# Attention in front of a mixture of experts: flat key tiles, and softmax sums from a column of ones

## The chip, the cores and the metric

The kernel runs on one core of one Trainium2 chip. The metric is the device time of one execution in microseconds (us), the median of several runs. Names of engines: PE is TensorE, PEld its weight loads, DVE VectorE, ACT ScalarE, POOL GpSimd, SP SyncE, which here only issues DMAs.

## What is computed

Batch 4, 8 heads, 576 positions, head dimension 64; then a mixture of 8 experts over the 2304 tokens of width 512, with hidden width 1024 and one expert per token.

```
scores = q @ k^T / 8 + bias(i, j, head)      # bias: a small MLP of the positions alone
attn   = exp(scores - max);  attn = attn / (sum(attn) + 1e-09)
x      = attn @ v                            # reshaped to tokens x 512
e      = argmax of normalised x @ normalised expert_emb^T / tau
out    = gate * (relu(x @ w1[e]) @ w2[e])
```

The change lies in the attention alone: in how the keys are laid out and scaled, in how the row sums of the exponentials are formed, and in the numbers by which the order of the work is set.

## The kernel before

**Units.** The four batches are taken in two pairs (`pr`). Queries come in five chunks per pair: chunks 0 to 3 hold 128 queries of each batch, chunk 4 the 64 left over. A unit is one pair, one chunk and one head; the order is pair 0 with chunks 4, 0, 1, 2, 3, then pair 1 with chunks 0, 1, 2, 3, 4, each with 8 heads: 80 units. In chunk 4 two heads make one step (`two`), so there are 64 steps of full chunks and 8 double steps. A step (`unit`, L659) is: scores of both batches on PE (L692, 12 matmuls of 16 bit pieces, into PSUM tiles `s0` and `s1`), bias add with row extremum on DVE (L707), the exponential on ACT (L710), 9 transposes on PE (L721) with copies out of PSUM on ACT or DVE (L727), the product with the values on PE (L743, 40 matmul halves into PSUM tile `o`), and division by the sums on DVE.

**Sums.** In full chunks the exponential's instruction also adds up its row into `sums`; every second unit DVE adds 1e-9 and takes the reciprocal (L753, L754), which needs the exponentials alone, and then multiplies two units' products at once (L759). In chunk 4 the value tile's 65th column, which holds ones in all chunks (L464), is used: the product is 65 wide and its last column is the sum (L748 to L750). `o` is one PSUM bank with one buffer; a new one is begun every four units (L731), so it holds four units of 128 columns, or in chunk 4 two double steps of 130.

**Keys.** `load_k` brings keys of 4 heads and a batch pair in 10 DMAs into `kr`, 9 blocks of 64 columns: batch 0's four full blocks of 128 keys, batch 1's four, which begin at key 64, and a shared block with batch 0's last 64 keys and batch 1's first 64. There is one such buffer, filled four times (pair by half of the heads). `prep_k` takes the greatest magnitude (two reductions, L493, over 4 and 5 blocks), makes a power of two per head of it (L495 to L490), and per head writes an upper 16 bit piece (ACT, L514 and L516) and a lower one (DVE, three instructions at L520) into `khl`, in which the shared block stands twice. Ten transposes (L528) and one copy of 1280 columns (L531) make `kt`. For batch 1 the scores of its first 64 keys go to columns 448 to 511 of `s1`, the rest to 512 to 1023 (L688 to L692).

**Order.** All of this is handed to a list scheduler (`Sched`, L123) that runs when the kernel is built. Each operation has an engine or a choice of engines, an assumed duration, what it reads and writes, and a priority counted in units; the planner places operations by time and priority and writes each engine's queue in that order. The priorities are numbers at the file's head: `KLA`, `KLB`, `KHB`, `KH`, `KP0`, `KP1` for the keys' preparation, `KA`, `KB`, `QA`, `VA` for when loads may start, `oS` to `oX` for the parts of a unit, `oL` for the bias tiles' loads, `BL` to `BP0` for the making of the bias, `PACE` for how far loads may run ahead of the DMA queue, `PEN` for what a copy on DVE must gain over ACT, `FP`, `FQ`, `FINP`, `FINE`, `GEP` for the end of attention. `BBK` says how many steps of the bias of chunk 0 may use four PSUM banks in place of one.

Three parts of the whole follow each other: up to some 150 us the bias of all chunks is made beside the first units (L618 on DVE, L633 on PE); from there units alone up to some 367 us, with the second pair's keys prepared up to 234 us; then the tokens are dispatched and the experts run.

```
k = (2 * D + 2) * (u % 4 // 2) if two else 128 * (u % 4)
nc.scalar.activation(pp()[:, S_ * b:S_ * b + S_], sx(), AF.Exp, bias=mx()[:, b:b + 1], scale=-1.0, accum_out=None if two else sums()[:, h, b:b + 1])
```

Of the kernel before, what the change touches and what calls it, by code (L numbers as in the profile page):

```python
# [27 lines left out]
S_ = S  # L28
# [22 lines left out]
BBK = 6  # L51
KBS = 12
KA = 21
KB = 35
QA = 36
VA = 11
KLA = 9.369
KLB = 5.845
KHB = 0.818
KP0 = -5.658  # L60
KP1 = -3.883
KH = 5.81
QL1 = 9.937
QL0 = 51.383
BL1 = 12.618
BS1 = 1.935
BP0 = -10.567
PSB = 0
ALPHA = 20.886
# [3 lines left out]
PRLD = 90.243  # L73
# [17 lines left out]
STP, STPM = 12.256, 60.738  # L91
VP0 = 127.364
oL0 = -2.201
# [170 lines left out]
class Kern:  # L264
# [97 lines left out]
    def attention(self):  # L362
        with ExitStack() as tail, ExitStack() as cx:
# [13 lines left out]
            for n in ("sm_kz", "sm_wt", "sm_sums", "sm_mx", "sm_ri"):  # L377
                self.p[n], self.r[n] = self.p[n.split("_")[0]], Rot(sizes[n.split("_")[0]])
# [3 lines left out]
            self.d, self.banks_used = {}, 0  # L382

# [54 lines left out]
    def load_kv(self, src, pr, hh, t, tok, prio, after, apart=0):  # L438
        nc = self.nc
        hs = slice(4 * hh, 4 * hh + 4)  # L440
        for b in range(2):
            a = src[2 * pr + b, hs]

            def main(c, a=a, b=b):
                nc.sync.dma_start(t()[:, :, 4 * b + c, 0:D], a[:, 64 * b + 128 * c:64 * b + 128 * c + 128, :].rearrange("h p d -> p h d"))

            def tail(a=a, b=b):
                nc.sync.dma_start(t()[64 * b:64 * b + 64, :, 8 + b * apart, 0:D], a[:, 512 - 512 * b:576 - 512 * b, :].rearrange("h p d -> p h d"))

            for c in range(4):  # L450
                self.S.op([("SP", 550, lambda c=c, main=main: main(c))], [], [tok] + ([] if b else [tok + (0,)]), [t], prio, 600, after, PACE if after else None)
            self.S.op([("SP", 550, tail)], [], [tok], [t], prio, 365, after, PACE if after else None)

    def load_k(self, pr, hh, prio, after):
        t = self.d["kr", pr, hh] = self.buf("kr", [128, 4, 9, 64], pool="kraw")
        self.load_kv(self.i["k"], pr, hh, t, ("kr", pr, hh), prio, after)

    def load_v(self, pr, hh, prio, after):

        nc = self.nc  # L460
        t = self.d["v", pr, hh] = self.buf("v", [128, 4, 10, D + 1])

        def zero():
            nc.gpsimd.memset(t()[:, :, :, D], 1.0)  # L464
            nc.gpsimd.memset(t()[0:64, :, 9, :], 0.0)
            nc.gpsimd.memset(t()[64:128, :, 8, :], 0.0)

        self.S.op([("POOL", 600, zero)], [], [("v", pr, hh)], [t], prio, 0, after)
        self.load_kv(self.i["v"], pr, hh, t, ("v", pr, hh), prio, after, 1)

    def prep_k(self, pr, hh, prio, step):
# [20 lines left out]
        for b in range(2):  # L492
            S.op([("DVE", 1120 + 266 * b, lambda b=b: nc.vector.tensor_reduce(z(b), kr()[:, :, 4 * b:4 + 5 * b].rearrange("p h c d -> p h (c d)"), axis=AX.X, op=ALU.max, apply_absolute_value=True))], [tk + (0,)] + ([tk] if b else []), [tz], [kr, zb], prio)  # L493
# [7 lines left out]
        for h in range(4):  # L501

            khl = self.buf("khl", [128, 2, 5, 128], F16)
            kt = self.d["kt", pr, 4 * hh + h] = self.buf("kt", [128, 2, 640], F16)
            th = ("khl", pr, hh, h)

            def places(h=h, khl=khl):

                for b in range(2):
                    yield kr()[:, h, 4 * b:4 * b + 4], lambda x, b=b: khl()[:, x, 0:4, 64 * b:64 * b + 64]  # L510
                yield kr()[:, h, 8].unsqueeze(1).to_broadcast([128, 2, 64]), lambda x: khl()[:, x, 4].rearrange("p (r d) -> p r d", r=2)

            def upper(h=h, khl=khl, places=places):
                nc.scalar.activation(khl()[:, 0, 0:4].rearrange("p c (b d) -> p b c d", b=2), kr()[:, h, 0:8].rearrange("p (b c) d -> p b c d", b=2), AF.Copy, scale=zb()[:, 12 + h:13 + h])  # L514
                src, out = [*places()][2]
                nc.scalar.activation(out(0), src, AF.Copy, scale=zb()[:, 12 + h:13 + h])  # L516

            def lower(h=h, places=places):
                for src, out in places():
                    nc.vector.scalar_tensor_tensor(out(1), src, zb()[:, 12 + h:13 + h], out(0), ALU.mult, ALU.subtract)  # L520

            S.op([("ACT", 900, upper)], [tz + (2,), tk], [th], [kr, zb, khl], prio + step * h)
            S.op([("DVE", 1053, lower)], [th, tk, tz + (2,)], [th + (1,)], [kr, zb, khl], prio + step * h)
            tp, tt = self.buf("s1", [128, 1024]), ("ktp", pr, hh, h)

            def tr(khl=khl, tp=tp):
                for c in range(10):
                    nc.tensor.transpose(tp().bitcast(F16)[:, 128 * c:128 * c + 128], khl()[:, c // 5, c % 5], self.idh)  # L528

            def ev(e, kt=kt, tp=tp):  # L530
                (e.copy if e is nc.scalar else e.tensor_copy)(kt().rearrange("p x k -> p (x k)"), tp().bitcast(F16)[:, 0:1280])  # L531

            S.op([("PE", 590, tr)], [th + (1,)], [tt], [khl, tp], prio + step * h)
            S.op([("ACT", 1116, lambda ev=ev: ev(nc.scalar)), ("DVE", 750, lambda ev=ev: ev(nc.vector), PEN)], [tt], [("kt", pr, 4 * hh + h)], [tp, kt], prio + step * h)
# [124 lines left out]
    def unit(self, u):  # L659
# [36 lines left out]
        if h == 0:  # L696
            if not two:
                self.sums = self.buf("sums", [128, 8, 2], pool="sm_sums")
            self.x = self.buf("xt", [128, 2, DM], pool="x")
        sums, xt = self.sums if not two else None, self.x  # L700
        mx = self.buf("mx", [128, 2], pool="sm_mx")
        pp = self.buf("pp", [128, 2 * S_])
        for b in range(2):
            sx = self.buf("ss", [128, S_], pool="s")

            def bias(b=b, sx=sx):
                nc.vector.tensor_tensor_reduce(out=sx(), in0=ss[b]()[:, 448 * b:448 * b + S_], in1=bt(), scale=1.0, scalar=3.0e38, op0=ALU.add, op1=ALU.min, accum_out=mx()[:, b:b + 1])  # L707

            def exp(b=b, sx=sx):
                nc.scalar.activation(pp()[:, S_ * b:S_ * b + S_], sx(), AF.Exp, bias=mx()[:, b:b + 1], scale=-1.0, accum_out=None if two else sums()[:, h, b:b + 1])  # L710

            S.op([("DVE", 677, bias)], [("S", u, b), ("bt", u)], [("ss", w, b) for w in us], [ss[b], bt, mx, sx], p0 + oB)
            S.op([("ACT", 760 if not two else 668, exp)], [("ss", u, b)], [("p", u, b)], [mx, sx, pp] + ([] if two else [sums]), p0 + oP)
# [17 lines left out]
        if u % 4 == 0:  # L731
            self.o = self.buf("o", [128, 512])
        ob = self.o
        k = (2 * D + 2) * (u % 4 // 2) if two else 128 * (u % 4)

        def av():
            for b in range(2):
                for j in range(5):
                    for x in range(2):
                        y, to = (x, b) if two else (b, x)  # L740
                        hh, at = (h % 4 + b, k + (D + 1) * b) if two else (h % 4, k + D * b)
                        n = D + 1 if two else D
                        nc.tensor.matmul(ob()[64 * x:64 * x + 64, at:at + n], pts()[:, 8 if j == 4 else 4 * y + j, 64 * to:64 * to + 64], v()[:, hh, 8 + y if j == 4 else 4 * y + j, 0:n], start=j == 0, stop=j == 4, tile_position=(0, 64 * x))  # L743
# [7 lines left out]
        elif u % 2:  # L751
            ri = self.buf("ri", [128, 2, 2], pool="sm_ri")
            S.op([("DVE", 70, lambda: nc.vector.tensor_scalar(ri(), sums()[:, h - 1:h + 1], 1e-9, None, ALU.add))], [("p", u, b) for b in range(2)], [("ri", u)], [sums, ri], p0 + oX)  # L753
            S.op([("DVE", 75, lambda: nc.vector.reciprocal(ri(), ri()))], [("ri", u)], [("ri", u, 1)], [ri], p0 + oX)  # L754

            def norm():
                xb = ob()[:, k - 128:k + 128].rearrange("p (u b d) -> p u b d", u=2, b=2)
                xo = xt().rearrange("p b (h d) -> p h b d", d=64)[:, h - 1:h + 1]
                nc.vector.tensor_tensor(xo, xb, ri().unsqueeze(3).to_broadcast([128, 2, 2, 64]), ALU.mult)  # L759
# [805 lines left out]
```

## Time and profile before

| | us |
|---|---|
| median of 3 runs | 639.14 |
| lowest and highest run | 638.0, 639.54 |
| the profiled execution, its own time | 637.61 |
| its span, first to last instruction | 635.8 |

The rows come from the profiled execution. Its time is 1.81 us more than its span, and the median is 1.53 us above it. Busy time of an engine is the union of its instructions' spans; instructions of an engine overlap a little at their ends, so that starts tell more of what an instruction costs its engine than durations. In brackets at the end of a timeline row stands the idle time before it and what ended it.

### The profile page before, as it was taken

Reading aid. Unit: us, or ns where it says so; the run is one execution under the profiler, and the core shown is the slowest. Engines: PE = TensorE matmul, PEld = TensorE weight load, DVE = VectorE, ACT = ScalarE, POOL = GpSimd, SP = SyncE. Lnnn points to the kernel's source line nnn. Section 1 sums busy time; section 2 is a strip of 40 time slices with the busy share of each in tenths; the row PEclk is TensorE's granted clock in tenths of the full one; section 3 lists DMA queues with packets and bytes.
Section 4 is the critical chain, followed back from the end, with each engine's and each line's share of the span. In section 5 each row is a group of like instructions: output and inputs, shape, how many; then the busy total and the mean of one; then the engine's idle time right before and its main releaser. Section 6 shows DMA issues by size and latency. Waiting matters only on the chain.

```text
span 635.8 us, 20690 instructions
## 1 busy us (share of the span) xinstructions
PE 581.2 (91%) x7663; PEld 394.0 (62%) x7663; DVE 510.9 (80%) x1422; ACT 465.4 (73%) x975; POOL 151.9 (24%) x221
## 2 busy tenths in 40 slices
PE   8677798999998889999999889799999999999993
PEld 3234456576877667777878766664675478457741
DVE  7899998799878788798977863987868887987752
ACT  6576687798989789999999633768786678758400
POOL 4453553442102043132100155200000000000173
PEclk9797999999999989999999998899999999999997
DMA  7899667699799949777974649995599479749642
GB/s 182 240 245 273 141 174 179 180 251 224 184 214 133 203 100 239 167 169 210 178 202 90 167 113 304 161 191 175 147 228 210 155 178 228 213 146 209 110 191 96
DMA packets 169466, 117.61 MB, mean 185 GB/s; under 512 B 124791, under 2 KB 145527, under 8 KB 169362
## 3 DMA queue, kind: packets, MB, share of 16 engines
q1 hardware_dynamic: 162146, 91.07, 64.2%
q0 software_dynamic: 7216, 25.14, 13.4%
q8 instruction: 67, 1.10, 0.7%
q14 instruction: 37, 0.30, 0.2%
HBM read 74.88 MB, written 21.87 MB: 152 GB/s over the span
## 4 chain that ended last, share of the span: by engine, by line
PE 37%; issue 35%; DVE 7%; POOL 5%; DMA 3%; ACT 2%; SPq 1%; POOLq 0%; DVEq 0%; ACTq 0%
PE o L743 12%; PE t L721 9%; PE s L692 7%; POOL out L1387 3%; PE m L633 3%; DVE hid L618 2%; PE m L721 2%; DVE ss L707 2%; DMA macc<-xs,kept 2%; DMA kr<-in_k 1%; DVE khl L520 1%; POOL macc L1398 1%; PE o L764 1%; PE e L1046 1%; PE s L528 1%
## 5 line engine op out<-in xcount | busy, mean ns | idle before, releaser
L710 ACT ACTIVATE pp<-ss,mx 128x576 f32<-128x576 f32 x144 | 111.1, 783 | 10.4 <-DVE mx L707 10.4
L707 DVE CUSTOM_DVE_ANT_0 ss<-s,bt 128x576 f32<-128x576 f32 x144 | 103.7, 752 | 13.0 <-PE s L692 9.1
L743 PE MATMUL o<-v,pts 128*64 128x64 f32 (+1 forms) x2880 | 101.2, 226 | 2.0 <-DVE xt L750 1.1
L743 PEld LDWEIGHTS o<-v,pts 128*64 128x64 f32 x2880 | 91.2, 139 | 14.6 <-issue 7.5
L1382 PE MATMUL p<-w2s,mht 128*128 (+1 forms) x432 | 97.3, 379 | 0.8 <-DVE macc L1482 0.4
L1382 PE MATMUL p<-w1s,mxt 128*128 (+1 forms) x768 | 96.6, 273 | 0.1
L721 PE MATMUL t<-ident,pp 128*128 128x128 f32 x576 | 85.1, 283 | 4.5 <-ACT pp L710 4.4
L1382 PEld LDWEIGHTS <-mxt 128*128 128x128 f16 (+1 forms) x768 | 73.4, 99 | 17.9 <-issue 2.4
L727 ACT COPY pts<-t 128x512 f32<-128x512 f32 x135 | 74.6, 590 | 8.1 <-PE t L721 3.7
L721 PEld LDWEIGHTS t<-ident,pp 128*128 128x128 f32 x576 | 62.5, 142 | 18.5 <-ACT pp L710 8.6
L692 PE MATMUL s<-kt,qt 64*128 64x512 f16 (+3 forms) x960 | 69.1, 285 | 4.4 <-DVE mx L707 2.8
L1382 PEld LDWEIGHTS <-mht 128*128 128x128 f16 (+1 forms) x432 | 41.1, 99 | 51.3 <-issue 6.1
L1387 POOL DMA_INDIRECT out<-macc,kept x20 | 19.7, 986 | 206.0 <-DVE macc L1482 206.0
L618 DVE TENSOR_SCALAR hid<-L,thr 128x448 f32<-128x448 f32 (+17 forms) x128 | 61.5, 531 | 5.2 <-PE m L633 4.3
L692 PEld LDWEIGHTS <-qt 64*128 64x128 f16 (+1 forms) x960 | 33.9, 97 | 44.6 <-issue 17.2
L1482 DVE SCALAR_TENSOR_TENSOR macc<-p,aux,macc 128x512 f32<-128x512 f32 x60 | 45.0, 753 | 15.8 <-PE p L1382 9.3
L1337 ACT ACTIVATE junk<-raw 128x1024 bf16<-128x1024 f32 x50 | 52.4, 1049 | 4.2 <-DMA raw<-in_moe_w 2.6
L1444 ACT ACTIVATE h<-p 128x256 f16<-128x256 f32 x72 | 27.1, 382 | 30.5 <-PE p L1382 18.8
L1342 ACT ACTIVATE w1s<-raw,kept 128x1024 f16<-128x1024 f32 x31 | 35.5, 1149 | 15.4 <-DVE kept L1321 15.4
L1343 DVE SCALAR_TENSOR_TENSOR w1s<-raw,kept,w1s 128x1024 f16<-128x1024 f32 x32 | 40.9, 1290 | 0.2
L633 PE MATMUL m<-hid,wt 128*32 128x256 f32 (+16 forms) x240 | 32.7, 547 | 8.7 <-ACT pts L727 3.0
L568 POOL TENSOR_TENSOR qab<-qs,qab 128x512 f16<-128x512 f32 x20 | 24.5, 1223 | 53.7 <-DVE qab L567 35.6
(316 smaller groups left out, 968.3 us busy)
## 6 DMA issues: line engine op xcount, KB each, us to landing
raw<-in_moe_w SPq DMA_DIRECT2D x60, 512.0 KB, 4.5
bt<-bsc SPq DMA_DIRECT2D x64, 288.0 KB, 3.6
bsc<-stg POOLq DMA_DIRECT2D x31, 318.0 KB, 4.2
xs<-row POOLq DMA_DIRECT2D x16, 256.5 KB, 6.0
kr<-in_k SPq DMA_DIRECT2D x32, 128.0 KB, 3.4
v<-in_v SPq DMA_DIRECT2D x32, 128.0 KB, 4.5
q<-in_q SPq DMA_DIRECT2D x8, 512.0 KB, 5.5
bt<-bsc SPq DMA_DIRECT2D x16, 144.0 KB, 3.9
```

What stands on the lines that cost most here:

```text
L618: e.tensor_scalar(hid()[:, 0:N_], self.L[:, 0:N_], self.thr[:, t0 + x:t0 + x + 1], None, ALU.max)
L633: nc.tensor.matmul(m()[32 * x:32 * x + 32, 0:n], w(x), hx[x]()[:, a:a + n], start=True, stop=True, tile_position=(0, 32 * x))
L692: nc.tensor.matmul(ss[b]()[rows, col:col + (512 if main else 64)], qt()[r, 4 * xq + h % 4 + y, qs], k, start=xq + xk == 0, stop=xq == 1, t ...
L707: nc.vector.tensor_tensor_reduce(out=sx(), in0=ss[b]()[:, 448 * b:448 * b + S_], in1=bt(), scale=1.0, scalar=3.0e38, op0=ALU.add, op1=ALU. ...
L710: nc.scalar.activation(pp()[:, S_ * b:S_ * b + S_], sx(), AF.Exp, bias=mx()[:, b:b + 1], scale=-1.0, accum_out=None if two else sums()[:, ...
L721: nc.tensor.transpose(t()[:, 128 * k:128 * k + 128], pp()[:, lo + 128 * k:lo + 128 * k + 128], self.ident)
L727: (e.copy if e is nc.scalar else e.tensor_copy)(pts()[:, at:at + n].rearrange("p a b -> p (a b)"), t()[:, 0:128 * n])
L743: nc.tensor.matmul(ob()[64 * x:64 * x + 64, at:at + n], pts()[:, 8 if j == 4 else 4 * y + j, 64 * to:64 * to + 64], v()[:, hh, 8 + y if j ...
L1337: S.op([("ACT", 1050, lambda: nc.scalar.activation(out() if not own else dst(0), rv() if own else raw(), AF.Square, scale=2.0 ** (-8 if wh ...
L1343: S.op([("DVE", 1192, lambda: nc.vector.scalar_tensor_tensor(dst(1), rv(), zs(), dst(0), ALU.mult, ALU.subtract))], [t + (3,), t + (2,)] + ...
L1382: nc.tensor.matmul(out[c, 0:n], lhs[:, c], w[:, bass.ds(ev[s] + at, n)], start=start, stop=stop)
L1482: S.op([("DVE", 664, lambda a=a, r=r, p2=p2: v.scalar_tensor_tensor(a, p2(), r, a, ALU.mult, ALU.add))], [("p2", q, s), ("rs", q)], [("acc ...
```

## The change

Keys: one tile, [128, 4 heads, 5 blocks, 2 batches, 64], made once, with the upper half of block 4 set to zero once on POOL. Both batches begin at key 0, block by block. The loads stay 10 per filling, now block by block with the batches in turn; the first reduction takes 3 blocks of both batches (1536 columns, six loads), the second two (1024 columns). Per head one ACT and one DVE instruction of 640 columns write the pieces; `kt` has 576 columns per piece, and its copy 1152. Scores of both batches stand in columns 0 to 575 of their PSUM tiles. Values keep their layout.

Sums: no exponential adds up its row. The product with the values is 65 wide in all chunks. `o` is begun anew every two full units; the two small DVE instructions read the sums from `o`, and so wait for the products.

Order: most of the numbers at the file's head that belong to attention are new; the diff shows those that the prediction speaks of. The numbers of the experts' part stay, but for one load's (`PRLD`) and one preparation's (`WP`) that run beside the units.

```diff
-PEN, PACE = 241.474, 1874.692
+PEN, PACE = 312.013, 1398.701
-FP, FQ, FN, FO = 2.1, 41.904, 3, 12
-FINE, GEP = -5.91, 14.651
+FP, FQ, FN, FO = 17.704, 25.319, 3, 12
+FINE, GEP = 1.592, 2.539
-BBK = 6
+BBK = 8
-KA = 21
-KB = 35
-QA = 36
-VA = 11
-KLA = 9.369
-KLB = 5.845
-KHB = 0.818
+KA = 28
+KB = 19
+QA = 24
+VA = 22
+KLA = 12.578
+KLB = 6.382
+KHB = 1.878
...
+            self.raw_k = self.p["kraw"].tile([128, 4, 5, 2, 64], F32, name="kr")
+            self.nc.gpsimd.memset(self.raw_k[64:128, :, 4], 0.0)
...
+        for c in range(5):
+            for b in range(2):
+                n = 128 if c < 4 else 64
+                def load(c=c, b=b, n=n):
+                    nc.sync.dma_start(t()[0:n, :, c, b, :], self.i["k"][2 * pr + b, 4 * hh:4 * hh + 4, 128 * c:128 * c + n, :].rearrange("h p d -> p h d"))
+                self.S.op([("SP", 550, load)], [], [("kr", pr, hh)] + ([("kr", pr, hh, 0)] if c < 3 else []), [t], prio, 600 if c < 4 else 365, after, PACE if after else None)
...
-            S.op([("DVE", 1120 + 266 * b, lambda b=b: nc.vector.tensor_reduce(z(b), kr()[:, :, 4 * b:4 + 5 * b].rearrange("p h c d -> p h (c d)"), ...
+            S.op([("DVE", (1650, 1120)[b], lambda b=b: nc.vector.tensor_reduce(z(b), kr()[:, :, 3 * b:3 + 2 * b].rearrange("p h c b d -> p h (c b d)"), ...
...
+                nc.scalar.activation(piece(0), raw(), AF.Copy, scale=zb()[:, 12 + h:13 + h])
+                nc.vector.scalar_tensor_tensor(piece(1), raw(), zb()[:, 12 + h:13 + h], piece(0), ALU.mult, ALU.subtract)
...
+                (e.copy if e is nc.scalar else e.tensor_copy)(kt(), tp().bitcast(F16)[:, 0:1280].rearrange("p (x k) -> p x k", x=2)[:, :, 0:S_])
...
-                        col = 512 * b if main else 512 - 64 * b
+                        col = 0 if main else 512
-                            k = kt()[r, xk, 0:512] if main else kt()[r, xk, 512 + 64 * b:576 + 64 * b]
+                            k = kt()[r, xk, 0:512] if main else kt()[r, xk, 512:S_]
...
+                nc.scalar.activation(pp()[:, S_ * b:S_ * b + S_], sx(), AF.Exp, bias=mx()[:, b:b + 1], scale=-1.0)
...
-        if u % 4 == 0:
+        if u % (4 if two else 2) == 0:
             self.o = self.buf("o", [128, 512])
         ob = self.o
-        k = (2 * D + 2) * (u % 4 // 2) if two else 128 * (u % 4)
+        k = (2 * D + 2) * (u % 4 // 2 if two else u % 2)
...
-            S.op([("DVE", 70, lambda: nc.vector.tensor_scalar(ri(), sums()[:, h - 1:h + 1], 1e-9, None, ALU.add))], [("p", u, b) for b in range(2)], [("ri", u)], [sums, ri], p0 + oX)
+            xb = lambda: ob()[:, 0:4 * D + 4].rearrange("p (g d) -> p g d", d=D + 1)
+            S.op([("DVE", 70, lambda: nc.vector.tensor_scalar(ri(), xb()[:, :, D], 1e-9, None, ALU.add))], [("o", u - 1), ("o", u)], [("ri", u)], [ob, ri], p0 + oX)
```

## Rows read from the trace of the kernel before

**Rows 1.** Stretches: start:end length, then busy us (instructions) per engine, clock, DMA share, GB/s.
```profile
0.00:64.00 64.00, 47.52 (x442) 22.78 (x442) 55.84 (x145) 41.49 (x78) 27.75 (x56) 0.87 0.93 234
64.00:128.00 64.00, 57.18 (x777) 34.03 (x779) 56.95 (x146) 46.14 (x106) 31.86 (x49) 0.97 0.67 171
128.00:192.00 64.00, 63.09 (x1150) 47.51 (x1150) 55.52 (x191) 59.23 (x150) 13.88 (x23) 1.00 0.94 214
192.00:256.00 64.00, 56.15 (x948) 43.87 (x946) 51.94 (x168) 56.87 (x130) 17.56 (x26) 0.97 0.95 173
256.00:336.00 80.00, 79.14 (x1469) 62.60 (x1468) 68.80 (x233) 78.68 (x198) 15.96 (x20) 1.00 0.77 182
...
358.00:402.00 44.00, 37.04 (x433) 27.86 (x432) 26.81 (x129) 18.87 (x35) 23.33 (x24) 0.94 0.74 202
```

**Rows 2.** Groups by line and shape, with busy us, mean ns: bias add, exponential's accumulator.
```profile
L707 DVE CUSTOM_DVE_ANT_0 ss<-s,bt 128x576 f32<-128x576 f32 x144 | 103.7, 752 | 13.0 <-PE s L692 9.1 <-ACT pp L710 2.7 <-PE m L1315 0.6
...
L710 ACT ACTIVATION_READ_ACCUMULATOR pp<-ss,mx 128x1 f32 x128 | 26.0, 203 | 0.0
```

**Rows 3.** Timeline: exponentials with row sums (306) and without (342); start, us.
```profile
306.00 0.78 ACT L710 ACTIVATE pp<-ss,mx 128x576 f32<-128x576 f32 x1
...
306.75 0.77 ACT L710 ACTIVATE pp<-ss,mx 128x576 f32<-128x576 f32 x1
...
342.61 1.46 ACT L710 ACTIVATE pp<-ss,mx 128x576 f32<-128x576 f32 x2
```

**Rows 4.** Groups by line and shape: preparing the keys, and wider instructions of the same kinds.
```profile
L1343 DVE SCALAR_TENSOR_TENSOR w1s<-raw,kept,w1s 128x1024 f16<-128x1024 f32 x32 | 40.9, 1290 | 0.2
...
L531 ACT COPY kt<-s 128x1280 f16<-128x1280 f16 x15 | 18.5, 1230 | 4.5 <-PE s L528 4.3
L520 DVE SCALAR_TENSOR_TENSOR khl<-kr,kz,khl 128x256 f16<-128x256 f32 x32 | 17.9, 600 | 0.0
...
L832 DVE SCALAR_TENSOR_TENSOR row<-xt,rq,row 128x512 f16<-128x512 f32 x17 | 12.5, 740 | 0.0
...
L514 ACT ACTIVATE khl<-kr,kz 128x512 f16<-128x512 f32 x16 | 11.4, 715 | 1.6 <-DVE kz L486 1.6
...
L516 ACT ACTIVATE khl<-kr,kz 128x128 f16<-128x128 f32 x16 | 6.3, 391 | 0.0
L520 DVE SCALAR_TENSOR_TENSOR khl<-kr,kz,khl 128x128 f16<-128x128 f32 x16 | 6.1, 383 | 0.0
...
L493 DVE TENSOR_REDUCE kz<-kr 128x4 f32<-128x1280 f32 x4 | 5.9, 1482 | 3.5 <-DMA kr<-in_k 2.6 <-DMA xs<-opt 1.0
```

**Rows 5.** Timeline: one head's lower pieces undisturbed, and POOL's wait at the start.
```profile
4.53 0.72 POOL L596 TENSOR_TENSOR wt<-w2bd,sall 128x128 f32<-128x128 f32 x1 [3.22 <-DVE sall L301]
...
27.17 1.13 DVE L520 SCALAR_TENSOR_TENSOR khl<-kr,kz,khl 128x256 f16<-128x256 f32 x3
```

**Rows 6.** Chain that ended last, a load of the second pair's keys: start, us, what.
```profile
201.64 8.60 DMA kr<-in_k
```

**Rows 7.** Timeline of DVE: preparing the second pair's keys.
```profile
210.37 1.49 DVE L493 TENSOR_REDUCE kz<-kr 128x4 f32<-128x1280 f32 x1 [2.57 <-DMA kr<-in_k]
...
224.74 4.74 DVE L520 SCALAR_TENSOR_TENSOR khl<-kr,kz,khl 128x256 f16<-128x256 f32 x9
```

**Rows 8.** Groups by line and shape: the product with the values, 64 and 65 wide.
```profile
L743 PE MATMUL o<-v,pts 128*64 128x64 f32 x2560 | 90.1, 226 | 0.9 <-DVE xt L759 0.9
...
L743 PE MATMUL o<-v,pts 128*64 128x65 f32 x320 | 11.1, 224 | 1.1 <-DVE xt L750 1.1
```

**Rows 9.** Stretch 160:192, line 743 alone: length, PE busy us (instructions, 40 a unit), PEld busy.
```profile
160.00:192.00 32.00, 13.70 (x400) 12.46 (x400) 1.00 0.87 189
```

**Rows 10.** Timeline of chunk 4 of pair 0: sums from the product, division, next product.
```profile
58.46 0.15 DVE L748 TENSOR_SCALAR ri<-o 128x2 f32<-128x2 f32 x1
...
58.85 0.29 DVE L750 TENSOR_TENSOR xt<-o,ri 128x128 f32<-128x128 f32 x1
...
59.20 1.39 PE L743 MATMUL o<-v,pts 128*64 128x65 f32 x40 [0.37 <-DVE xt L750]
```

More of the change, by code (lines that the diff above doesn't have):

```diff
@@ L50 @@
 W1S, W2S, L2P = 3.942, 1.7, 22.604
-BBK = 6
+BBK = 8
 KBS = 12
-KA = 21
-KB = 35
-QA = 36
-VA = 11
-KLA = 9.369
-KLB = 5.845
-KHB = 0.818
[L60 to L67, printed above, removed]
+KA = 28
[5 more added lines that the diff above has]
+KHB = 1.878
+KP0 = -3.305
+KP1 = -0.024
+KH = 3.17
+QL1 = 9.378
+QL0 = 31.347
+BL1 = 4.813
+BS1 = 2.685
+BP0 = -7.269
 PSB = 0
-ALPHA = 20.886
+ALPHA = 21.894
 ALPHB = 5.392
@@ L72 @@
 PRE = 2
-PRLD = 90.243
+PRLD = 80
 AVD, PTW = 1315, 0.5
@@ L90 @@
 XX0 = 2
-STP, STPM = 12.256, 60.738
-VP0 = 127.364
-oL0 = -2.201
+STP, STPM = 13.068, 60.738
+VP0 = 119.56
+oL0 = -15.599
 SZ = {}
@@ L376, in attention @@
                 self.r[n] = Rot(k)
-            for n in ("sm_kz", "sm_wt", "sm_sums", "sm_mx", "sm_ri"):
+            for n in ("sm_kz", "sm_wt", "sm_mx", "sm_ri"):
                 self.p[n], self.r[n] = self.p[n.split("_")[0]], Rot(sizes[n.split("_")[0]])
@@ L436, in buf, with load_kv @@
         return Buf(self.r[pool or name], lambda: p.tile(shape, dt, name=name))
-    def load_kv(self, src, pr, hh, t, tok, prio, after, apart=0):
+    def load_kv(self, src, pr, hh, t, tok, prio, after):
         nc = self.nc
@@ L447, in tail @@
             def tail(a=a, b=b):
-                nc.sync.dma_start(t()[64 * b:64 * b + 64, :, 8 + b * apart, 0:D], a[:, 512 - 512 * b:576 - 512 * b, :].rearrange("h p d -> p h d"))
+                nc.sync.dma_start(t()[64 * b:64 * b + 64, :, 8 + b, 0:D], a[:, 512 - 512 * b:576 - 512 * b, :].rearrange("h p d -> p h d"))
             for c in range(4):
-                self.S.op([("SP", 550, lambda c=c, main=main: main(c))], [], [tok] + ([] if b else [tok + (0,)]), [t], prio, 600, after, PACE if after else None)
+                self.S.op([("SP", 550, lambda c=c, main=main: main(c))], [], [tok], [t], prio, 600, after, PACE if after else None)
             self.S.op([("SP", 550, tail)], [], [tok], [t], prio, 365, after, PACE if after else None)
     def load_k(self, pr, hh, prio, after):
-        t = self.d["kr", pr, hh] = self.buf("kr", [128, 4, 9, 64], pool="kraw")
-        self.load_kv(self.i["k"], pr, hh, t, ("kr", pr, hh), prio, after)
+        nc, t = self.nc, Buf(self.r["kraw"], lambda: self.raw_k)
+        self.d["kr", pr, hh] = t
+        for c in range(5):
[4 more added lines that the diff above has]
+                self.S.op([("SP", 550, load)], [], [("kr", pr, hh)] + ([("kr", pr, hh, 0)] if c < 3 else []), [t], prio, 600 if c < 4 else 365, after, PACE if after else None)
     def load_v(self, pr, hh, prio, after):
@@ L468, in load_v @@
         self.S.op([("POOL", 600, zero)], [], [("v", pr, hh)], [t], prio, 0, after)
-        self.load_kv(self.i["v"], pr, hh, t, ("v", pr, hh), prio, after, 1)
+        self.load_kv(self.i["v"], pr, hh, t, ("v", pr, hh), prio, after)
     def prep_k(self, pr, hh, prio, step):
@@ L492, in prep_k @@
         for b in range(2):
[L493 removed]
+            S.op([("DVE", (1650, 1120)[b], lambda b=b: nc.vector.tensor_reduce(z(b), kr()[:, :, 3 * b:3 + 2 * b].rearrange("p h c b d -> p h (c b d)"), axis=AX.X, op=ALU.max, apply_absolute_value=True))], [tk if b else tk + (0,)], [tz], [kr, zb], prio)
         S.op([("DVE", 180, lambda: nc.vector.tensor_tensor(z(0), z(0), z(1), ALU.max))], [tz], [tz + (3,)], [zb], prio)
@@ L503, in prep_k, with upper, lower @@
             khl = self.buf("khl", [128, 2, 5, 128], F16)
-            kt = self.d["kt", pr, 4 * hh + h] = self.buf("kt", [128, 2, 640], F16)
+            kt = self.d["kt", pr, 4 * hh + h] = self.buf("kt", [128, 2, S_], F16)
             th = ("khl", pr, hh, h)
[L507 to L523, printed above, removed]
+            raw, piece = lambda h=h: kr()[:, h].rearrange("p c b d -> p (c b d)"), lambda x, khl=khl: khl()[:, x].rearrange("p c k -> p (c k)")
+            def upper(h=h, raw=raw, piece=piece):
+                nc.scalar.activation(piece(0), raw(), AF.Copy, scale=zb()[:, 12 + h:13 + h])
+            def lower(h=h, raw=raw, piece=piece):
+                nc.vector.scalar_tensor_tensor(piece(1), raw(), zb()[:, 12 + h:13 + h], piece(0), ALU.mult, ALU.subtract)
+            S.op([("ACT", 620, upper)], [tz + (2,), tk], [th], [kr, zb, khl], prio + step * h)
+            S.op([("DVE", 780, lower)], [th, tk, tz + (2,)], [th + (1,)], [kr, zb, khl], prio + step * h)
             tp, tt = self.buf("s1", [128, 1024]), ("ktp", pr, hh, h)
@@ L530, in ev @@
             def ev(e, kt=kt, tp=tp):
-                (e.copy if e is nc.scalar else e.tensor_copy)(kt().rearrange("p x k -> p (x k)"), tp().bitcast(F16)[:, 0:1280])
+                (e.copy if e is nc.scalar else e.tensor_copy)(kt(), tp().bitcast(F16)[:, 0:1280].rearrange("p (x k) -> p x k", x=2)[:, :, 0:S_])
             S.op([("PE", 590, tr)], [th + (1,)], [tt], [khl, tp], prio + step * h)
-            S.op([("ACT", 1116, lambda ev=ev: ev(nc.scalar)), ("DVE", 750, lambda ev=ev: ev(nc.vector), PEN)], [tt], [("kt", pr, 4 * hh + h)], [tp, kt], prio + step * h)
+            S.op([("ACT", 1020, lambda ev=ev: ev(nc.scalar)), ("DVE", 690, lambda ev=ev: ev(nc.vector), PEN)], [tt], [("kt", pr, 4 * hh + h)], [tp, kt], prio + step * h)
     def load_q(self, pr, hh, prio, after, after2):
@@ L696, in unit @@
         if h == 0:
-            if not two:
-                self.sums = self.buf("sums", [128, 8, 2], pool="sm_sums")
             self.x = self.buf("xt", [128, 2, DM], pool="x")
-        sums, xt = self.sums if not two else None, self.x
+        xt = self.x
         mx = self.buf("mx", [128, 2], pool="sm_mx")
@@ L706, in bias @@
             def bias(b=b, sx=sx):
-                nc.vector.tensor_tensor_reduce(out=sx(), in0=ss[b]()[:, 448 * b:448 * b + S_], in1=bt(), scale=1.0, scalar=3.0e38, op0=ALU.add, op1=ALU.min, accum_out=mx()[:, b:b + 1])
+                nc.vector.tensor_tensor_reduce(out=sx(), in0=ss[b]()[:, 0:S_], in1=bt(), scale=1.0, scalar=3.0e38, op0=ALU.add, op1=ALU.min, accum_out=mx()[:, b:b + 1])
             def exp(b=b, sx=sx):
-                nc.scalar.activation(pp()[:, S_ * b:S_ * b + S_], sx(), AF.Exp, bias=mx()[:, b:b + 1], scale=-1.0, accum_out=None if two else sums()[:, h, b:b + 1])
+                nc.scalar.activation(pp()[:, S_ * b:S_ * b + S_], sx(), AF.Exp, bias=mx()[:, b:b + 1], scale=-1.0)
             S.op([("DVE", 677, bias)], [("S", u, b), ("bt", u)], [("ss", w, b) for w in us], [ss[b], bt, mx, sx], p0 + oB)
-            S.op([("ACT", 760 if not two else 668, exp)], [("ss", u, b)], [("p", u, b)], [mx, sx, pp] + ([] if two else [sums]), p0 + oP)
+            S.op([("ACT", 668, exp)], [("ss", u, b)], [("p", u, b)], [mx, sx, pp], p0 + oP)
         pts = self.buf("pts", [128, 9, 128], pool="pt")
@@ L740, in av @@
                         y, to = (x, b) if two else (b, x)
-                        hh, at = (h % 4 + b, k + (D + 1) * b) if two else (h % 4, k + D * b)
-                        n = D + 1 if two else D
-                        nc.tensor.matmul(ob()[64 * x:64 * x + 64, at:at + n], pts()[:, 8 if j == 4 else 4 * y + j, 64 * to:64 * to + 64], v()[:, hh, 8 + y if j == 4 else 4 * y + j, 0:n], start=j == 0, stop=j == 4, tile_position=(0, 64 * x))
+                        hh, at = h % 4 + (b if two else 0), k + (D + 1) * b
+                        nc.tensor.matmul(ob()[64 * x:64 * x + 64, at:at + D + 1], pts()[:, 8 if j == 4 else 4 * y + j, 64 * to:64 * to + 64], v()[:, hh, 8 + y if j == 4 else 4 * y + j, :], start=j == 0, stop=j == 4, tile_position=(0, 64 * x))
         S.op([("PE", AVD, av)], [("pts", u), ("v", pr, h // 4)], [("o", w) for w in us], [pts, v, ob], p0 + oA, mode=2)
```

15 lines of the change are left out of this document (7 added, 8 removed).

## The prediction

> **What bounds the kernel now.** I read the stretches first [rows 1], since a mean over the span says nothing here. There are four kinds. Up to 128 us DVE is the busiest (55.84 and 56.95 of 64 us) and PE stands idle for 64 - 47.52 = 16.5 and 64 - 57.18 = 6.8 us, with a granted clock of 0.87 and 0.97. From 128 to 192 us, and from 256 to 336 us, PE is busy for 63.09 of 64 and 79.14 of 80 us: there only less work on PE can help, and the change takes none away. From 192 to 256 us PE idles again, 64 - 56.15 = 7.9 us: that is where the second pair's keys are made ready. From 358 to 402 us, the dispatch, PE idles 7.0 us. The experts behind it are untouched. So whatever the change saves on ACT and DVE can be cashed in the first stretch and at the second pair's keys, and the most that can be had there is 16.5 + 6.8 + 7.9 = 31 us of idle PE.
>
> The rest [rows 2 to 10] I read in this order: the groups by line, for how long an instruction is; the timeline, for what it costs its engine when issued back to back, which is less; and the chain of waits with the timeline beside it, for what PE waits for at the second pair's keys and at the turn of `o`.
>
> **Row sums off the exponential.** The page of groups shows 128 reads of the accumulator with 26.0 us [rows 2], which looks like 26 us saved on ACT. The timeline says less: with row sums one exponential starts 306.75 - 306.00 = 0.75 us after the other, the read lying over its neighbours; without, two take 1.46 us together, and one alone 0.78, so that the second starts 0.68 after the first [rows 3]. That is 0.07 us each, 128 x 0.07 = 9 us of ACT, spread over 64 units. Most of it lies where PE is full [rows 1], and is covered by PE's queue. In the stretch 256 to 336 ACT is full beside PE (78.68 of 80), so that a late copy now and then will come sooner; PE's idle time there is 0.9 us in all. I take -0.5 us; ends 0 and -9.
>
> **The column of ones.** The product with the values becomes 65 wide. Chunk 4 runs it already, at 224 ns a matmul where 64 columns take 226 [rows 8]: no cost. The end above is one column in 64 of such a product's 1.37 us [rows 9], 64 units: +1.4 us. The Trainium skill, "TensorE: Matmul & The Clock Gate", Part 2, says that a matmul's time goes by the number of moving columns; by it the sum would hold that +1.4, and by the rows 0. The rows decide, as they are the same product.
>
> **Keys.** Per head DVE runs one instruction of 640 columns in place of 256 + 256 + 128. By the means the old three take 2 x 600 + 383 = 1583 ns, undisturbed 1.13 us [rows 4, 5]; the new one, between 740 ns at 512 columns and 1290 at 1024 [rows 4], comes to 740 + 128 x 550/512 = 878 ns. It saves 0.25 to 0.70 us; I take 0.45, between the ends, as about half of the old ones run undisturbed. Against that the reductions cover 2560 columns where they covered 2304: 256 more at 1482 ns for 1280, +0.30 us per filling [rows 4]. One filling, four heads: 4 x 0.45 - 0.30 = 1.5 us of DVE less (0.7 to 2.5). ACT's pieces go from 715 + 391 = 1106 ns [rows 4] to about 715 + 128 x (715 - 391)/384 = 823, -0.28 us a head; the copy of `kt` from 1280 to 1152 columns, a tenth of 1230 ns at most, -0.12.
> Two fillings fall before 128 us. DVE is busy there for 112.8 of 128 us, so about two thirds of 2 x 1.5 should reach the end: **-2.0 us** (0 to -5.0). At the second pair's keys, three heads' lower pieces run in one block of 4.74 us [rows 7]; with 878 ns each it is 2.6: -2.1, and by the undisturbed price 3 x 0.25 = -0.75. I take **-1.5 us**.
> The ten loads of a filling move the same bytes from the same queue. The first reduction now waits for six loads instead of four, but DVE has bias work to do meanwhile. The zeroing of the tile's corner, once, on POOL, falls into the 3.22 us that POOL waits at the start [rows 5]; without that cover it would cost one memset ahead of the first bias, under 1 us.
>
> **The wait for `o`.** New is that the two small DVE instructions wait for the product, not for the exponentials, and that the single bank turns over every two units instead of four: 32 turns in place of 16 in the full chunks. Behind a waiting product stand, on PE's queue, the next unit's transposes and scores. Chunk 4 shows the same chain: the first small instruction starts at 58.46, the division at 58.85, the next product at 59.20, 0.37 us of that being PE idle [rows 10]. So a turn takes 0.74 us from DVE's start; the division there has 128 columns and takes 0.29 us, so with 256 a turn takes 1.03 at most, and more if DVE is in the middle of something else. In the present order PE waits 0.9 us in all for divisions in full chunks and 1.1 in chunk 4 [rows 8], the latter with four turns, and the planner knows of the buffer and puts other PE work between. I take +1.5 us: 32 turns at 0.05. The ends are 0 and 32 turns x 0.37 = 12.
>
> **The new order.** Every step with a new priority takes along its DMAs: key loads, value and query loads, bias tiles all move in SP's queue. What I can price is one spot: a key load of the second pair takes 8.60 us [rows 6] among value loads, and DVE waits 2.57 us for it in front of everything queued behind [rows 7]. In the new order these keys' preparation stands 3.2 units earlier (`KLA`), loads run less far ahead (`PACE`), and values may start sooner (`VA`). If the wait goes, the bias add that stands behind the reduction is next, 0.75 us of it [rows 2]; I take half of 2.57 as gained, **-1.3 us** (0 to -2.57), and a further **-1.0 us** for the start, where ACT, relieved, can take copies off DVE (0 to -5, as PE's idle 23 us there allow; the other way +4, about one unit of 3.2 us lost [rows 9]). For the end of attention, whose steps are re-timed, I take 0 of its 7.0 idle us [rows 1], 2 either way.
>
> **Sum.** -0.5 + 0 - 2.0 - 1.5 + 1.5 - 1.3 - 1.0 = -4.8 us against the profiled execution's own 637.61: 632.8. The median of the runs is 1.53 above it, so **634.3 us**, say 634.
>
> **Rivals.** *All covered.* The savings lie where PE is full, and the order only trades one stall for another: 639 us, give or take 1.9. For it speaks that over 144 of the 336 us of units PE has next to no idle time; against it, that the key steps sit where PE does idle.
> *The bank turns too late: slower.* One mechanism: DVE works in order, and the small instructions and the division may stand behind a bias add of 0.75 us [rows 2]. Then every turn of `o` shows 0.37 us as in chunk 4, 32 x 0.37 = 12 us, against my 1.5; with the other terms, -6.3 + 11.8 = +5.5 us: 645. It decides from 6.3/32 = 0.2 us a turn. Against it: with ten units in 32 us, each product taking 1.37 [rows 9], 3.2 - 1.37 = 1.8 us lie between one product's end and the next one's start, just room for 1.03 + 0.75. For it: while one bank turns, nothing of the next pair can be written. The Trainium skill, "Perfetto Trace Analysis", Optimizing Tensor Performance, Matmuls, asks for just the opposite, groups that rotate through different banks so that emptying one overlaps the next; by that rule this is the likely outcome, and the wait in chunk 4 agrees with it.
> *Not what it says.* If the reads of the accumulator stayed, or the 26 us were all on the path, the time would be 635, or 639 - 26 = 613 and less; the starts in the timeline exclude the latter.
>
> **Chances.** About 0.3%, 1.9 us, is what a measurement of this kernel can tell from no change, so "same" is 637.2 to 641.1. Forecast (faster) 0.64; all covered 0.20; slower 0.16, most of it the bank. The range takes in the lower ends of the key terms and of the start (-4.8 - 3.0 - 4.0, about 627, rounded down by the end's 2 to 625) and above the covered case to 641; it leaves out the bank's full price.
>
> **What would show it.** No read of the accumulator under the exponential, starts 0.68 apart; the khl row on DVE with 16 instructions near 880 ns; products at about 225 ns; stretches 0:128 and 192:256 with less idle PE, and full ones as long as before. Wrong would be: waits of PE for the division above 0.2 us a turn; the same idle time at the second pair's keys under another name, a DMA most likely; or a gain that comes from the dispatch, which I put at nothing.

## The result, and the profile after

The changed kernel takes **631.95 us** (median of 6 runs, 627.37 to 634.89) where the kernel before, run beside it, took 639.18: a ratio of 0.9896, 95% interval 0.9865 to 0.9928, 7.2 us less. The profiled execution took 631.98 us, 5.6 less than that of before, with a span of 630.1. Measured again, on two further occasions and chips, the ratio was 0.9955 [0.9927, 0.9983] and 0.9943 [0.9909, 0.9977]. So the gain is 0.5 to 1%, and 634 of 639, 0.8%, lies inside that. Here and below a median is of all runs, while a ratio leaves out single runs that lie over 1.5% above the fastest of their kernel.

The stretches, with the columns of [rows 1]; the fifth ends at 330 us here, at 336 there:

```profile
0.00:64.00 64.00, 48.53 (x416) 22.38 (x417) 52.67 (x124) 38.67 (x67) 26.30 (x56) 0.87 0.88 224
64.00:128.00 64.00, 59.07 (x853) 35.50 (x850) 60.85 (x150) 47.49 (x95) 33.30 (x54) 1.00 0.82 198
128.00:192.00 64.00, 63.27 (x1175) 48.67 (x1168) 54.90 (x189) 57.75 (x123) 15.05 (x23) 1.00 0.94 209
192.00:256.00 64.00, 57.34 (x985) 45.45 (x981) 49.22 (x153) 52.04 (x97) 17.94 (x27) 0.97 0.77 161
256.00:330.00 74.00, 73.69 (x1371) 58.62 (x1369) 63.67 (x216) 73.05 (x149) 11.92 (x16) 1.00 0.82 189
```

PE's idle time is 15.5, 4.9 and 6.7 us in the first two stretches and the fourth, where it was 16.5, 6.8 and 7.9: 4.1 us less, in the places the prediction had named. That is one execution of each kernel: in the two later profiles of the changed kernel (second and third set below) PE idles 10.2 and 10.7 us from 192 to 256. The full stretches stay full. The last matmul of the products with the values starts at 361.6 us, 5.0 earlier than the 366.6 of before.

The groups by line and shape, with the columns of [rows 2] (code lines have moved: exponential L711, product L743, lower key pieces L523, division L759):

```profile
L711 ACT ACTIVATE pp<-ss,mx 128x576 f32<-128x576 f32 x144 | 107.8, 794 | 11.8 <-DVE mx L708 11.2 <-DVE rg L887 0.6
...
L743 PE MATMUL o<-v,pts 128*64 128x65 f32 x2880 | 101.0, 225 | 1.3 <-DVE xt L759 1.1 <-DVE rq L885 0.2
...
L523 DVE SCALAR_TENSOR_TENSOR khl<-kr,kz,khl 128x640 f16<-128x640 f32 x16 | 14.6, 934 | 0.5 <-ACT khl L520 0.5
L759 DVE TENSOR_TENSOR xt<-o,ri 128x256 f32<-128x256 f32 x32 | 13.6, 424 | 1.0
```

No read of the accumulator stands under the exponential. The product is 65 wide throughout and a matmul of it takes 225 ns, against 226 and 224 in [rows 8]. These spans overlap; but the 40 matmuls of one step together take the same too, 1.39 us as the median, 64 wide before and 65 wide after. By the number of columns, the rule of the Trainium skill ("TensorE: Matmul & The Clock Gate", Part 2), it would have been 1.4 us more in all; the row shows none of it.

ACT's timeline (start, us, what): two exponentials take 1.42 to 1.56 us together, 1.47 as the mean of 49 such pairs. So a second one starts 0.68 us after the first; the 51 neighbours with row sums in the kernel before stand 0.77 apart.

```profile
177.29 1.45 ACT L711 ACTIVATE pp<-ss,mx 128x576 f32<-128x576 f32 x2
...
266.14 1.52 ACT L711 ACTIVATE pp<-ss,mx 128x576 f32<-128x576 f32 x2
```

DVE's timeline at the second pair's keys, beside [rows 7]:

```profile
200.35 1.22 DVE L503 TENSOR_REDUCE kz<-kr 128x4 f32<-128x1024 f32 x1 [2.50 <-DMA kr<-in_k]
210.37 0.88 DVE L523 SCALAR_TENSOR_TENSOR khl<-kr,kz,khl 128x640 f16<-128x640 f32 x1
211.50 2.58 DVE L523 SCALAR_TENSOR_TENSOR khl<-kr,kz,khl 128x640 f16<-128x640 f32 x2
216.10 0.88 DVE L523 SCALAR_TENSOR_TENSOR khl<-kr,kz,khl 128x640 f16<-128x640 f32 x1
```

The wait for the key load has not gone: 2.50 us where it was 2.57. It only comes 10 us earlier, and the last lower piece ends at 217.0 instead of 229.5. One piece takes 0.88 us undisturbed. In the two later profiles of the changed kernel the wait for the key load is 5.3 and 4.9 us.

What TensorE waited for between 64 and 372 us (us in all, times, longest), the rows for divisions, L759 in full chunks and L750 in chunk 4:

```profile
PE t L819 <- DVE xt L750: 1.6, 2, 1.2
PE o L743 <- DVE xt L759: 1.1, 1, 1.1
```

Of the bank's 32 turns in full chunks one shows, with 1.1 us (second row; L819 in the first row transposes attention's output for the tokens).

### The profile page after: what moved, and what is told of

It is laid out like the page before. It is cut to its first block, busy times and chain, and to the rows that moved or that the text cites. A ratio compares the mean times of both kernels' runs of the same rounds, so it can differ in the third digit from the quotient of the medians.

```text
span 630.1 us, 20541 instructions
## 1 busy us (share of the span) xinstructions
PE 579.6 (92%) x7663; PEld 393.2 (62%) x7663; DVE 506.5 (80%) x1379; ACT 452.4 (72%) x842; POOL 150.0 (24%) x222
## 4 chain that ended last, share of the span: by engine, by line
issue 34%; PE 15%; POOL 5%; ACT 4%; DVE 1%; DMA 1%; POOLq 0%; ACTq 0%; DVEq 0%
PE o L743 5%; PE t L722 4%; PE s L695 3%; POOL out L1387 3%; ACT pts L728 2%; ACT pp L711 2%; POOL macc L1398 1%; DMA macc<-xs,kept 1%; PE m L722 1%; POOL macc L1029 0%; PE e L1046 0%; ACT w1s L1337 0%; PE o L764 0%; PE e L1039 0%; POOL row L894 0%
## 5 line engine op out<-in xcount | busy, mean ns | idle before, releaser
L711 ACT ACTIVATE pp<-ss,mx 128x576 f32<-128x576 f32 x144 | 107.8, 794 | 11.8 <-DVE mx L708 11.2
L743 PE MATMUL o<-v,pts 128*64 128x65 f32 x2880 | 101.0, 225 | 1.3 <-DVE xt L759 1.1
L743 PEld LDWEIGHTS o<-v,pts 128*64 128x64 f32 x2880 | 91.2, 139 | 16.9 <-issue 9.6
L728 ACT COPY pts<-t 128x512 f32<-128x512 f32 x137 | 76.4, 599 | 11.7 <-PE t L722 8.6
L621 DVE TENSOR_SCALAR hid<-L,thr 128x448 f32<-128x448 f32 (+17 forms) x128 | 65.0, 563 | 4.4 <-PE m L636 3.9
L1342 ACT ACTIVATE w1s<-raw,kept 128x1024 f16<-128x1024 f32 x32 | 36.9, 1156 | 13.5 <-DVE kept L1321 13.5
L1445 DVE SCALAR_TENSOR_TENSOR h<-p,h 128x256 f16<-128x256 f32 x72 | 30.1, 422 | 8.1 <-ACT h L1444 7.3
```

Of the source, the lines that this page charges most:

```text
L621: e.tensor_scalar(hid()[:, 0:N_], self.L[:, 0:N_], self.thr[:, t0 + x:t0 + x + 1], None, ALU.max)
L728: (e.copy if e is nc.scalar else e.tensor_copy)(pts()[:, at:at + n].rearrange("p a b -> p (a b)"), t()[:, 0:128 * n])
L743: nc.tensor.matmul(ob()[64 * x:64 * x + 64, at:at + D + 1], pts()[:, 8 if j == 4 else 4 * y + j, 64 * to:64 * to + 64], v()[:, hh, 8 + y i ...
```

## The experiments

Times of different chips can't be set side by side: the kernel before took 653.02 us on the chip of the first set, 640.75 on that of the second, 656.00 on that of the third. Each ratio is to the kernel before on the same chip.

**First set: code and order apart.** The planner's result can be written into a kernel as a list, because both kernels hand it the same 2078 operations. In short (not the literal lines):

```diff
-        for i in sorted(range(n), key=lambda i: (start[i], i)):
+        for i in written_order:      # and the engine of each operation from the same list
```

Before's code in the new order:

> The code of before, its operations issued in exactly the order and on the engines of the changed kernel (the order is written out; the two kernels have the same 2078 operations). Before 639.2 us, the change 632.0. If the gain is the order's, this comes near the change: 632 to 635. If it is the code's (shorter key pieces, no row sums), this stays near before, 637 to 641, or above it, since an order made for shorter steps is then followed by longer ones. My forecast had -2.3 us for the order and -2.5 for the rest, so 636 to 637.

Measured 659.58 us, **1.0067** [1.0034, 1.01].

The changed code in before's order (the two small DVE instructions moved directly ahead of the division, and one reduction one place later, since they now need more):

> The changed code in the order of before, which is altered only where it must be: in the full chunks the two small instructions on the sums stand directly ahead of the division, and one reduction of the keys stands one DVE instruction later. If the gain is the code's: 632 to 635. If it is the order's: 637 to 640. By my forecast's terms (-0.5, -2.0, -1.5 and +1.5 for the turning bank) 636 to 637.

Measured 660.66 us, **1.0106** [1.007, 1.0142]. So neither half is faster alone; each is slower than before by more than its interval.

Where the changed code loses in before's order can be read in part. DVE's waits there, from 40 to 380 us, hold this one (us in all, times, longest):

```profile
DVE kz L521 <- DMA kr<-in_k: 5.9, 1, 5.9
```

It is a first reduction of the second pair's keys, which now needs six loads instead of four; TensorE waits 6.3 us behind it. At 224 us 33.3 steps' products are through, where the kernel before, on its own chip, had 36.0. So this run prices a wait for loads along with the saved work, and doesn't tell what the saved work alone is worth in the old order.

Before without its row sums (ones stand in place of the sums):

> Before, without the row sums of the full chunks' exponentials: the sums are set to ones, so the attention is left undivided; order and everything else as before. By the starts in the timeline this frees 9 us of ACT, of which I put 0.5 us on the path: 638 to 639.5. If ACT is a bound of its own beside PE, it gives 3 us or more: 636 or less.

Measured 697.77 us, which tells nothing of the row sums: undivided rows send the tokens to other experts, and the experts' part runs another branch, with 22 scatters of the output instead of 20. Its attention ends with a last product at 371.1 us; there is no profile of the kernel before from that chip to set beside it. What row sums cost in the old order stays open.

The change with the row sums on again, their results unused:

```diff
-... AF.Exp, bias=mx()[:, b:b + 1], scale=-1.0)
+... AF.Exp, bias=mx()[:, b:b + 1], scale=-1.0, accum_out=None if two else self.spare[:, (2 * h + b):(2 * h + b) + 1])
```

> The change, with the row sums of the full chunks' exponentials taken again, into a tile that nobody reads; order as in the change. If freed ACT time is covered by PE: 632 to 633. If the new order lives on it: 635 to 641 (128 x 0.07 = 9 us at most).

Measured 655.66 us, 1.0028 [0.9992, 1.0065]: with the row sums back no gain is left. The change itself was not in this set, which the next one mends.

**Second set: the saved work, put back one by one**, all in the new order.

> The changed kernel once more, so that the others of this set have it on the same chip. 0.987 to 0.993 of before, as in its first comparison.

Measured 637.84 us, 0.9955 [0.9927, 0.9983].

> The change with the row sums of the full chunks' exponentials taken again, into a tile nobody reads; order as in the change. In the first set this was 1.003 of before, without the change itself beside it. If row sums are covered by PE, as I forecast (0.5 us): within 0.3% of the change. If the new order has no room for them: 5 to 9 us slower than the change, near 1.000 of before.

Measured 645.22 us, 1.008 [1.0049, 1.0111]: **7.4 us** over the change.

```diff
-                nc.vector.scalar_tensor_tensor(piece(1), raw(), ...)
+                for lo, hi in ((0, 256), (256, 512), (512, 640)):
+                    nc.vector.scalar_tensor_tensor(piece(1)[:, lo:hi], raw()[:, lo:hi], ...)
```

and the upper piece on ACT in two, 0 to 512 and 512 to 640:

> The change with the keys' pieces written as before, two ACT and three DVE instructions a head with the old widths, in the change's order and layout. By my terms 0.25 to 0.7 us a head on DVE and 0.28 on ACT; -2.0 - 1.5 us of the forecast come from this and the like, so 2 to 4 us slower than the change. If the key steps are covered: within 0.3% of it.

Measured 640.14 us, 0.9989 [0.9951, 1.0026]: 2.3 us over the change, though the two intervals overlap.

> Both put back at once, in the change's order: what is left of the gain is the order's. If the two add up: the sum of their prices. If the order alone carries the gain: within 0.4% of the change; if it carries none or costs, as the old code in the new order on the first chip (1.007 of before) suggests: 1.000 to 1.010 of before.

Measured 646.78 us, 1.0093 [1.0061, 1.0126]: 8.9 us over the change, near 7.4 + 2.3. What is left of the change with both costs back, flat tiles, column of ones and new order, is 6.0 us slower than the kernel before.

Where the row sums take their 7.4 us the progress of the units tells: with and without them 56.0 and 56.2 steps' products are through at 304 us, 59.8 and 61.0 at 320, 68.0 and 70.0 at 352. In between stands this, DVE's timeline of the kernel with row sums, then the chain that ended last:

```profile
304.04 0.43 DVE L571 CAST qab<-qs 128x512 f16<-128x512 f32 x1 [3.69 <-DMA qt<-qab]
```
```profile
294.79 8.95 DMA qt<-qab
```

DVE stands still until a transposing load has read the one buffer `qab` (query pieces). Without row sums the same wait was 1.1 us. So the 7.4 us could be this wait, not ACT.

The wait belongs to the new order. With both costs put back, from 302 to 319 us:

```profile
DVE qab L573 <- DMA qt<-qab: 4.8, 1, 4.8
```

Over the whole span DVE's waits for `qab` come to 0.3 us in the kernel before and to none in the changed code in before's order; in the new order they come to 6.7 us with before's code, 5.5 with row sums, 3.9 with split pieces, 6.2 with both, and 0.7 and 2.2 in the change itself (first profile and second set; the third follows).

**Third set: that wait taken away.** A second buffer for `qab`, order as it is:

```diff
-SZ = {}
+SZ = {"qab": 2}
```

> The changed kernel as it is, as the mark for the three beside it. In its earlier profile VectorE's cast of qab waited 1.1 us at 299 us for the transposing load of the queries before it. Expected again: 0.990 to 0.997 of the kernel before.

Measured 652.27 us, 0.9943 [0.9909, 0.9977].

> The changed kernel in its own order, with two buffers for qab in place of one, so that no cast has to wait for a transposing load to have read the buffer. In the changed kernel these waits are 0.7 to 2.2 us of VectorE in all. Theory (the wait hurts only if it is long): 0 to 1 us faster than the change. Rival (VectorE's waits of that kind pass on to TensorE one for one): up to 2.2 us faster.

Measured 647.45 us, **0.9889** [0.9844, 0.9935], 4.8 us under the change by the medians, 3.5 by the ratios. The intervals overlap by a little, so that it is likely faster than the change, and surely than the kernel before. What a long wait does can be read off the profiled execution of the change on this chip (657.59 us, one of its longest), which has the wait at its worst. DVE, TensorE, and the stretch 304:320 of that kernel:

```profile
304.53 0.43 DVE L570 CAST qab<-qs 128x512 f16<-128x512 f32 x1 [5.40 <-DMA qt<-qab]
```
```profile
306.01 0.37 PE L695 MATMUL s<-kt,qt 64*128 64x512 f16 x1 [3.56 <-DVE mx L708]
306.69 1.59 PE L695 MATMUL s<-kt,qt 64*128 64x512 f16 x11 [0.31 <-DVE mx L708]
```
```profile
304.00:320.00 16.00, 13.68 (x191) 10.28 (x192) 11.38 (x38) 10.88 (x20) 1.77 (x2) 0.79 0.50 109
```

and the same stretch with two buffers, where no cast waits:

```profile
304.00:320.00 16.00, 16.00 (x308) 13.02 (x302) 14.32 (x49) 15.28 (x32) 2.31 (x3) 1.00 0.63 181
```

5.4 us of DVE became 3.6 us of TensorE and then a granted clock of 0.79 over these 16 us, in which 11 matmuls of the scores took 1.59 us where 12 take 0.91 in the first profile of the change. My bound, "up to 2.2 us faster", came from executions in which the wait was short. How much of the 3.5 to 4.8 us is such long waits is not shown: in the change's two other profiles the longest was 0.7 and 1.1 us.

> As the run with two buffers for qab, with the row sums on every full exponential again. With one buffer the row sums cost 7.4 us, and the profile then had a wait of 3.7 us at 300 us: VectorE for the transposing load of qab. Theory A (half of the 7.4 us is that wait, the rest is ScalarE's own time late in the attention): the row sums cost 3 to 5 us over the kernel with two buffers, and the wait is gone. Theory B (all of it is ScalarE's time, 128 x 0.07 = 9 us, most of it on the path): still 6 to 9 us. Theory C (all of it is the wait): under 1.5 us.

Measured 654.95 us, 0.9983 [0.9949, 1.0016]: 7.5 us over the kernel with two buffers by the medians, 6.2 by the ratios. **Theory B is nearest**: without that wait the row sums cost about as much as with it. The last product with the values begins 6.5 us later with them (361.4 and 367.9 us), and did so by 6.7 with one buffer (363.9 and 370.6). Theory C is out; the intervals are too wide to shut out the upper part of theory A. So the wait is not what the row sums cost. The chain that ended last, 256 to 360 us, by engine and line: the kernel before, then two buffers, then two buffers with row sums (exponential and copies out of PSUM on ACT are L710 and L727, L729 and L746, L730 and L747):

```profile
by line: PE o L743 30.4%; PE t L721 23.5%; PE s L692 20.0%; PE o L764 3.8%; PE m L721 3.7%; DVE ss L707 3.7%; issue 3.3%; ACT pp L710 1.6%; DVE rq L1076 1.1%; ACT pts L727 0.6%; ACT row L830 0.6%; PE m L874 0.6%; PE m L873 0.6%; DVE opt L91
```
```profile
by line: PE o L761 29.0%; PE t L740 23.7%; PE s L713 16.6%; ACT pp L729 6.2%; ACT pts L746 6.1%; PE m L740 3.5%; issue 3.2%; PE o L782 1.9%; ACT row L845 1.0%; PE m L890 1.0%; PE m L891 1.0%; PE m L892 1.0%; ACT w1s L1360 0.9%; DVE ss L726 
```
```profile
by line: PE o L762 19.4%; ACT pp L730 18.9%; PE t L741 15.8%; ACT pts L747 13.7%; PE s L714 9.0%; issue 7.0%; ACT w1s L1356 2.2%; PE m L741 2.1%; ACT row L846 1.7%; ACT row L849 1.5%; DVE ss L727 1.4%; ACT w1s L1361 1.2%; PE o L783 1.0%; PE
```

In the kernel before, row sums and all, exponential and copies hold 2.2% of the chain; with two buffers in the new order 12.3% without row sums and 32.6% with them. The changed kernel's first profile has 11.4%, and before's code in the new order 23.9%, which points to the order. But the changed code in before's order has 10.7%, with no row sums at all, so the 2.2% of one execution is not what the old order always gives. ACT's busy time over the whole span is 452.3 and 463.4 us without and with: 11.1 us, of which 6 to 7.5 reach the end.

> The code of the change, planned anew with the numbers of the kernel before, so that the planner sets the order for the new parts but no priority is changed. Theory (code and numbers need each other, as the two frozen orders had it): 1.000 to 1.012 of the kernel before. Rival (the new parts bring the gain and the numbers are a trimming): 0.990 to 0.997, as the change itself.

Measured 674.04 us, **1.0277** [1.0232, 1.0321]: worse than the theory's upper end; the rival falls. At 208 us it stands level with the change on that chip (32.0 steps each); then come the second pair's keys, and by 224 us it has 33.0 steps against 36.0. TensorE's stretch there:

```profile
192.00:256.00 64.00, 50.80 (x782) 39.52 (x784) 46.62 (x141) 43.17 (x80) 15.40 (x23) 0.89 0.81 145
```

13.2 us idle, where the change on that chip has 10.7 (53.26 busy). Why numbers tuned for other costs do that much harm in this place was not taken apart.

## Why the prediction was right, and where it was not

The direction and the size of the gain were right, and in the first pair of profiles its places; two terms of the sum were wrong by about 7 us each, in opposite directions.

- **Row sums, -0.5 us: mis-sized.** 7.4 us measured, 6.2 to 7.5 with two buffers. The price per exponential was near (0.07 worked out, 0.68 and 0.77 between starts, so 0.09). What failed is the sentence "Most of it lies where PE is full, and is covered by PE's queue". That fits the order of before, in which ACT holds 2.2% of the late chain. But the changed kernel doesn't run in that order, and in its own ACT is a second bound beside PE from 256 us on. The busy share, which the prediction had seen, doesn't tell the two apart: ACT is as full in either (78.68 of 80 us before, 73.05 of 74 after); the chain does. That the new plan puts ten more copies on ACT (137 of 512 columns and 68 of 128, before 135 and 60) goes with it, but was not tried by itself. What row sums cost in the old order no run shows, so that the order makes the difference is argued from the chain. The end of -9 held the truth; the taken value was read off the schedule of before.
- **The new order, -1.3 and -1.0 us: wrong sign as a term by itself.** With the saved work put back the new order (with flat tiles and the column of ones) is 6.0 us slower than before, and before's code in it 0.67%. The sum had left out a wait that this order brings: DVE's for `qab`, 6.2 and 6.7 us in those two profiles against 0.3 before. With two buffers the row sums alone put back give 0.9983; with the pieces' 2.3 us on top that would be some 1 us slower than before instead of 6.0 (an estimate across two chips; no run has both costs and two buffers). "If the wait goes" failed too: DVE still waits 2.5, 5.3 and 4.9 us for the key load in the three profiles of the change, and TensorE behind it 2.0, 4.7 and 4.4. The keys' preparation ends 12.5 us earlier in the first of them and TensorE idles 1.2 us less from 192 to 256; in the other two it idles more there than the 7.9 of before on its own chip, and idle time kept by a DMA was a sign of being wrong that the prediction had named.
- **Keys, -2.0 and -1.5 us.** 2.3 us measured for the pieces, too uncertain to be told from 3.5; 878 ns worked out for the lower piece against 0.88 us undisturbed (934 as a mean). Part of it is earned early: with the split pieces 11.2 steps are through at 128 us, without 12.0. That DVE has other work while the first reduction waits for its six loads, put at nothing, held at the second pair's keys in the new order; in the old one that wait cost 5.9 us of DVE there.
- **Column of ones, 0: right.** 225 ns.
- **The wait for `o`, +1.5 us: right.** One wait of 1.1 us in 32 turns, 0.03 us a turn where the rival decided at 0.2; the schedule puts other TensorE work between two products. By the rule on rotating banks (the Trainium skill, "Perfetto Trace Analysis", Optimizing Tensor Performance, Matmuls) the single bank should have shown; this trace does not bear it out.
- **Dispatch and end, 0.** The lead over before is 5.0 us at the last product with the values, 7.9 at the last gather of the dispatch (392.1 against 400.0) and 5.8 at the first scatter of the output (595.4 against 601.2). So the dispatch gained 2.9 us, more than the 2 I allowed, and the experts gave 2.1 back: 0.8 in all, in this one pair of executions.
- *All covered* (within 0.3% of before) is refuted by the first ratio; the other two only show that there is a gain. It is refuted in its mechanism by the row sums. And *not what it says* is refuted by the missing reads of the accumulator.

So the total of -4.8 (-5.6 in the profiles, -7.2, -2.9 and -3.7 in the three pairs of medians) came out right because two errors cancel: the saved work was worth 8.9 us where I had 4.0, and the rest of the change cost 6.0 where I had it earn 2.3 - 1.5 = 0.8. That is luck: no reason in the prediction ties the one to the other.

## What to carry to other kernels

Whether an engine's saved time counts must be asked of the schedule that the change will run in, not of the one in the trace: where a change brings a new order along, an engine that looks covered can be the second bound there, and the trace of before need not show it. Price code and order together, or bound both by the saved engine time in full (here 128 x 0.09 = 11.5 us, of which 6 to 7.5 came). And look for a single buffer that a slow transfer empties: its longest wait was 0.7, 1.1 and 5.4 us in three executions of one kernel, each on another occasion, and a second buffer took it away.

## What the runs showed of the hardware that I had not expected

- A transposing load of 128 x 1024 halves held its source buffer for 6.4 us in one execution (issued at 289.58, the waiting cast at 295.99), 9.2 in another and 11.1 in a third (293.40 to 304.53), with the same two bias tiles of 288 KB behind it in the queue. In the kernel before, those from 150 us on took 3.2 to 4.8 us from issue to landing, where the profile gives it. What draws it out was not settled.
- The same kernel before took 639.18 us in the first measurement and 653.02, 640.75 and 656.00 us on the three chips of the sets, up to 2.6% apart, more than anything this change did. Only ratios from one chip can be compared.
- An instruction of 203 ns on the page, the read of the accumulator, costs its engine 0.09 us, since it lies over its neighbours, and yet 128 of them moved the end by 6 to 7.5 us in the new order.
